# Two more batches of q transposed by DMA, in an attention and channel-mix kernel on one core

## The chip, the cores and the metric

The kernel runs on one core of one Trainium2 chip. The metric is the device time of one execution in microseconds. One execution was also taken by the hardware profiler, and all views of the trace are of that one.

## The reference

The program computes an attention over 32 memory slots and feeds its result to a channel mix. Sizes are batch B = 8, heads H = 8, sequence S = 576, head size D = 64, memory slots M = 32, model width 512, hidden width 1024. Cut to what matters:

```python
a = softmax(phi, axis=2)                       # (8, 8, 576, 32)
k_m = einsum('bhsm,bhsd->bhmd', a, k)
v_m = einsum('bhsm,bhsd->bhmd', a, v)
attn = softmax(scale * q @ k_m.T)              # q: (8, 8, 576, 64)
x = (attn @ v_m), heads side by side           # (8, 576, 512)
x_prev = x shifted by one token
xk = mu_k * x + (1 - mu_k) * x_prev
xr = mu_r * x + (1 - mu_r) * x_prev
out = sigmoid(xr @ w_r) * (relu(xk @ w_k)**2 @ w_v)
```

Inputs and output are float32; the kernel's matmuls are on bf16.

## The kernel before

The work is cut into named steps. A step is written `who:name`. For a batch b (0 to 7), `b:exp` takes exp of phi; `b:kv` (or `k` and `v` apart) forms k_m and v_m with TensorE (L237); `b:z` the sums; `b:nk`, `b:nv` the scaling on VectorE; `b:tk` the transposed keys; `b:q0` and `b:q1` transpose q with 18 TensorE matmuls each (L339) and copy the result to the tile qT (L343); `b:qx` does the same by two DMA transposes that SyncE issues (L315), one for each half of the partitions; `b:s0`, `b:s1` are the scores (L358); `b:l0` to `b:l3` the sums of the second softmax (L372); `b:w0`, `b:w1` the weights; `b:x0`, `b:x1` the values (L288); then the mixing steps. Batches 0 and 1 use variants with halves (`qh0`, `hn0`, `ht0`, `mr0`, `mk0`) to begin early. For the channel mix, `c<chunk>:<fi>` is one of eight hidden tiles of a chunk of 512 tokens (L520 to L528), `g:<t>` the gate of a tile of 128 tokens (L543), and `o:<t>` its output (L565 to L568), which ends in two stores that SyncE issues (L505).

Nothing is reordered by a scheduler: the list PLAN is one written-out order, and each step appends its instructions to the queues of the engines that it uses, each of which runs in its own order. A word `p:...` issues an early load, `b:load` (L291) issues the loads of batch b + 2, in the order that LOADS names. All loads of batches 1 to 7 are issued by GpSimd, cast float32 to bf16 on the way for q, k and v, and wait until their buffer is free: k, v, q and phi have two buffers each, for even and odd batches. The tile qT has three buffers, the output tile o four, and all PSUM tiles share eight banks. In before, `qx` is used for batches 6 and 7, and `q0`, `q1` for 1 to 5.

The DMAs of one kind share eight semaphores in turn, so that a DMA also waits for the landing of the DMA eight places ahead of it. `b:hold` (L263) is not used in before. The lines that a sentence can't say:

```python
def cross_q():
    for hg in range(2):
        nc.sync.dma_start_transpose(out=q_tile()[:, hg],
                                    in_=qs[b % 2][ROWS[hg]].rearrange("p n d -> p (n d)"))
def hold():
    spare = work.tile([1, 2], BF16, name="spare", tag="spare", bufs=1)
    nc.gpsimd.tensor_copy(spare, st["qT"][0:1, :, 0, 0])
```

`keep_busy` (L191, step `busy2`) issues two matmuls on zeros at the start; `mub` and `mu` (L198, L206) prepare the mixing vectors.

Of the kernel before, what the change touches and what calls it, by code (L numbers as in the profile page):

```python
# [15 lines left out]


PLAN = [
    "p:q:0a p:k:0b 0:exp1 0:exp0 0:k0c 0:z 0:qh0 0:k1c 0:hn0 0:ht0 0:s0 p:q:0b 0:hn1 p:v:0a 0:qh1 0:l0 0:ht1 0:l1",
    "0:s1 0:mub p:v:0b 0:l2 p:wr:0-4 p:wk:0-4 0:h1z 0:v0c 0:h0z 0:nr0 0:v1c p:phi:1 0:h2z 0:l3 0:y1 0:y0 p:wk:4-8",  # L20
    "0:h3z 0:nr1 0:busy2 0:y2 0:y3 0:nk0 0:nk1 0:mr0 0:mr1 0:mk0 0:mk1 c0:2a c0:0a g:2 1:exp c0:3a c0:2b c0:5b c0:4b",
    "g:3 1:z c0:6a g:0 p:k:1 1:k 1:nk c0:6b p:q:1 c0:7b c0:0b c0:3b 1:q0 1:q1 0:mu 1:tk c0:5a c0:1a c0:4a p:v:1 1:s1",
    "1:s0 c0:1b 1:v 1:l2 1:l0 c0:7a 1:nr0 p:wv:0-2 p:wv:2-4 1:nk0 1:h0z 1:l3 1:l1 1:h2z 1:nr1 1:h1z 1:h3z g:1 o:3a",
    "1:y2 1:y3 o:2a 1:nk1 1:y0 1:y1 o:2b o:3b 1:mk1 o:0a 1:mk0 1:mr0 c1:0 c1:2 c1:4 1:mr1 g:4 c1:6 c1:3 0:load 2:exp",
    "g:5 2:q0 2:q1 o:1a 7:load 2:z 2:kv 2:nk 2:nv o:0b 2:tk c1:1 2:s1 2:s0 c1:7 c1:5 2:l0 2:l2 2:l1 2:l3 2:r0z 2:r1z",
    "2:w0 2:w1 o:1b o:5 o:4 1:load 3:exp 2:x0 3:q0 g:6 3:z 3:q1 3:kv 2:x1 3:nk g:7 3:nv 3:tk 2:dd 2:k0d g:8 3:s0 3:s1",
    "2:load 2:k2d o:6 4:exp o:7 2:r0d 3:l0 c2:1 c2:5 3:l3 3:l2 4:z 3:l1 c2:0 3:r1z 3:w1 3:r0z 3:w0 c2:4 2:r2d c2:2",
    "c2:3 c2:7 3:x1 4:kv 3:load c2:6 3:x0 4:nk 4:nv g:10 3:dd 3:k0d g:11 3:k2d g:9 5:exp 4:tk 4:q1 4:q0 o:9 o:10 c3:7",
    "c3:0 o:8 5:z 4:s0 5:kv 4:load 3:r0d 4:s1 5:q1 6:exp 5:q0 6:qx 5:nk c3:5 c3:4 4:l1 3:r2d 4:l2 c3:3 5:nv 4:l3 4:l0",
    "5:tk 4:r1z c3:6 g:12 c3:2 6:z 6:kv 6:nv 5:s0 4:r0z 5:load 5:s1 4:w1 4:w0 c3:1 g:13 6:nk o:11 g:14 6:tk 4:x0 o:13",  # L30
    "4:x1 g:15 4:dd o:12 5:l3 4:k0d 5:l0 5:l1 5:r0z o:14 5:l2 4:k2d g:16 7:exp 4:r0d 5:r1z o:15 c4:1 c4:3 7:z 7:kv",
    "6:s1 5:w0 5:w1 6:s0 c4:5 c4:0 5:x0 7:nv 4:r2d 7:nk c4:2 6:l1 c4:4 c4:6 6:l2 c4:7 7:qx 6:l3 5:x1 5:dd g:18 5:k2d",
    "g:19 7:tk 6:l0 g:17 o:18 5:k0d 6:r1z o:16 o:19 7:s1 6:r0z 7:s0 c5:3 c5:1 c5:7 6:w0 g:20 7:l2 c5:2 6:w1 7:l0 7:l1",
    "c5:6 7:l3 5:r2d c5:0 c5:5 c5:4 7:r1z 5:r0d 6:x1 o:17 6:x0 g:21 7:r0z 6:dd 6:k2d o:20 o:21 7:w1 g:22 6:k0d g:23",
    "7:w0 o:23 o:22 6:r2d c6:2 7:x1 c6:5 c6:1 6:r0d 7:x0 c6:4 g:24 7:dd c6:0 6:load c6:7 c6:3 c6:6 g:25 g:26 7:k0d",
    "7:r0d 7:k2d g:27 o:25 o:24 o:26 c8:0 c7:5 c8:6 7:r2d g:28 o:27 g:29 c7:6 c7:0 c7:4 c8:2 g:30 c7:1 c7:2 c7:7 c7:3",
    "g:31 c8:7 c8:4 o:29 c8:3 o:28 o:31 g:32 c8:5 o:30 c8:1 g:33 g:34 o:33 g:35 o:32 o:34 o:35",
]

LOADS = {None: ("phi", "k", "v", "q"), 2: ("phi", "k", "q", "v"), 3: ("phi", "k", "q", "v"), 4: ("phi", "k", "q", "v")}  # L40
PRE = "k:0a id:"
SUMS = ()

# [6 lines left out]
def kernel(  # L50
# [64 lines left out]
    def load_batch(b):  # L115
        for what in LOADS.get(b, LOADS[None]):
            if what == "phi":
                load_phi(b, nc.gpsimd)
            elif what == "q":
                load_q(b)  # L120
            else:
                load_rows(kvs[b % 2][:, "kv".index(what)], (k, v)["kv".index(what)][b])
# [498 lines left out]
```

## Time and profile before

| what | value |
|---|---|
| median of three runs (lowest, highest) | 209.61 us (209.15, 209.96) |
| the profiled execution | 208.39 us, span 206.6 us, TensorE clock 0.999 |
| TensorE busy | 193.9 us, 94% of the span |
| ScalarE, VectorE, GpSimd busy | 159.5, 135.4, 29.4 us |
| bytes moved by DMA | 32.49 MB, of which 20.91 MB on the queue that GpSimd feeds |
| TensorE transposes of q, L339 | 180 matmuls, 190 ns each by the trace |
| VectorE copies of them, L343 | 18, 451 ns each |
| DMA transposes, L315 | 4 |

The span runs from the first to the last instruction; the execution's own time is 1.8 us longer. Matmuls are pipelined, so the sum of the means of single matmuls is more than the time that a group takes; the chain that ended last shows the latter. The trace gives the load of the DMA engines in slices and in windows, by queue: queue 0 is the one that GpSimd feeds, queue 1 the one that SyncE feeds. A DMA's time "to landing" runs from its issue.

### The profile page before, as it was taken

Reading aid. Unit: us, or ns where it says so; the run is one execution under the profiler, and the core shown is the slowest. Engines: PE = TensorE matmul, PEld = TensorE weight load, DVE = VectorE, ACT = ScalarE, POOL = GpSimd, SP = SyncE. Lnnn points to the kernel's source line nnn. Section 1 sums busy time; section 2 is a strip of 40 time slices with the busy share of each in tenths; the row PEclk is TensorE's granted clock in tenths of the full one; section 3 lists DMA queues with packets and bytes.
Section 4 is the critical chain, followed back from the end, with each engine's and each line's share of the span. In section 5 each row is a group of like instructions: output and inputs, shape, how many; then the busy total and the mean of one; then the engine's idle time right before and its main releaser. Section 6 shows DMA issues by size and latency. Waiting matters only on the chain.

```text
span 206.6 us, 5609 instructions
## 1 busy us (share of the span) xinstructions
PE 193.9 (94%) x2269; PEld 103.5 (50%) x2269; DVE 135.4 (66%) x364; ACT 159.5 (77%) x314; POOL 29.4 (14%) x45
## 2 busy tenths in 40 slices
PE   0499999999999999999999999999999999999992
PEld 0355676746555545466445764444434444444451
DVE  1129445866478989988749779487978944533232
ACT  3256899978778999978999799989878955882570
POOL 7652422201414102150000000000000000000000
PEclk9999999999999999999999999999999999999999
DMA  6999999999999999999999850502260062004335
GB/s 161 173 204 262 210 208 202 261 230 285 215 273 239 256 279 213 260 231 307 208 157 211 126 87 16 124 17 52 54 154 0 0 152 54 0 0 112 91 71 135
DMA packets 29274, 32.49 MB, mean 157 GB/s; under 512 B 6704, under 2 KB 24384, under 8 KB 29248
## 3 DMA queue, kind: packets, MB, share of 16 engines
q0 software_dynamic: 17392, 20.91, 53.8%
q1 hardware_dynamic: 11088, 10.37, 23.3%
q10 hardware_dynamic: 768, 0.85, 1.3%
q8 instruction: 18, 0.29, 0.6%
q14 instruction: 8, 0.07, 0.1%
HBM read 38.28 MB, written 9.44 MB: 231 GB/s over the span
## 4 chain that ended last, share of the span: by engine, by line
PE 92%; DMA 3%; POOL 1%; DVE 1%; issue 1%; POOLq 0%; DVEq 0%
PE pk L520 31%; PE pv L565 31%; PE pr L543 15%; PE kvps L237 4%; DMA kv<-in_k_dram 3%; PE mxps L288 2%; PE zps L372 2%; PE scps L358 2%; PE qtps L339 2%; PE nops L288 2%; PE zps L247 1%; PE ktps L301 1%; PE mub L200 1%; PE qtps L326 1%; DVE o L567 0%
## 5 line engine op out<-in xcount | busy, mean ns | idle before, releaser
L520 PE MATMUL pk<-xkT,wk 128*128 128x512 bf16 (+4 forms) x352 | 69.0, 341 | 0.0
L565 PE MATMUL pv<-wv,sq 128*128 128x512 bf16 (+1 forms) x328 | 66.2, 353 | 0.0
L528 DVE TENSOR_TENSOR sq<-rl 128x512 bf16<-128x512 bf16 (+5 forms) x104 | 32.7, 341 | 33.3 <-ACT rl L524 32.5
L524 ACT ACTIVATE rl<-pk 128x512 bf16<-128x512 f32 (+3 forms) x80 | 42.9, 560 | 13.4 <-PE pk L520 10.6
L520 PEld LDWEIGHTS <-wk 128*128 128x128 bf16 x352 | 32.7, 98 | 27.8 <-issue 1.6
L565 PEld LDWEIGHTS <-sq 128*128 128x128 bf16 x328 | 31.5, 98 | 29.9 <-issue 0.5
L543 PE MATMUL pr<-wr,xrT 128*128 128x512 bf16 x144 | 35.8, 380 | 0.0
L567 DVE TENSOR_TENSOR o<-sg,pv 128x512 f32<-128x512 f32 (+1 forms) x41 | 24.9, 620 | 15.0 <-PE pv L565 8.7
L548 ACT ACTIVATE sg<-pr 128x512 f32<-128x512 f32 x36 | 21.5, 610 | 8.8 <-PE pr L543 8.8
L543 PEld LDWEIGHTS <-xrT 128*128 128x128 bf16 x144 | 13.5, 98 | 14.8 <-issue 0.2
L550 ACT ACTIVATE sg<-sg 128x1024 f32<-128x1024 f32 x18 | 19.0, 1057 | 0.6
L551 ACT ACTIVATE sg<-sg 128x1024 f32<-128x1024 f32 x18 | 19.0, 1057 | 0.6
L401 ACT CAST x<-nops 128x320 bf16<-128x320 f32 (+1 forms) x48 | 15.7, 419 | 2.4 <-PE nops L288 2.3
L237 PE MATMUL kvps<-kv,em 64*32 64x128 bf16 (+1 forms) x720 | 8.7, 218 | 7.8 <-DMA kv<-in_k_dram 7.8
L423 DVE TENSOR_SCALAR mu_d<-diff,mu 128x576 bf16<-128x576 bf16 x48 | 15.5, 364 | 0.1
L362 ACT ACTIVATE e<-scps 128x320 bf16<-128x320 f32 (+1 forms) x32 | 11.0, 415 | 4.3 <-PE scps L358 4.2
L389 DVE TENSOR_TENSOR atn<-e,lz 128x576 bf16<-128x576 bf16 (+2 forms) x20 | 12.0, 631 | 1.4 <-ACT lz L382 1.3
L377 ACT ACTIVATE lz<-zps 128x320 f32<-128x320 f32 (+1 forms) x32 | 11.7, 413 | 0.8 <-PE zps L372 0.8
L237 PEld LDWEIGHTS <-em 64*32 64x32 bf16 x720 | 7.5, 95 | 8.9 <-ACT em L225 6.1
L225 ACT ACTIVATE em<-ph 128x1152 bf16<-128x1152 f32 (+1 forms) x9 | 9.4, 1056 | 2.3 <-DMA ph<-in_phi_dram 2.3
L382 ACT ACTIVATE lz<-lz 128x576 f32<-128x576 f32 (+2 forms) x20 | 11.1, 587 | 0.1
L413 DVE TENSOR_TENSOR diff<-x 128x1024 bf16<-128x1024 bf16 (+1 forms) x18 | 9.0, 552 | 2.4 <-ACT x L401 2.4
(65 smaller groups left out, 143.7 us busy)
## 6 DMA issues: line engine op xcount, KB each, us to landing
out_dram<-o SPq DMA_DIRECT2D x61, 128.0 KB, 2.4
ph<-in_phi_dram POOLq DMA_DIRECT2D x7, 576.0 KB, 15.7
kv<-in_k_dram POOLq DMA_DIRECT2D x7, 576.0 KB, 15.8
q<-in_q_dram POOLq DMA_DIRECT2D x7, 576.0 KB, 17.9
kv<-in_v_dram POOLq DMA_DIRECT2D x7, 576.0 KB, 19.3
out_dram<-o SPq DMA_DIRECT2D x18, 64.0 KB, 5.5
wk<-in_moe_w_k_dram POOLq DMA_DIRECT2D x2, 512.0 KB, 14.8
wv<-in_moe_w_v_dram POOLq DMA_DIRECT2D x2, 512.0 KB, 20.3
```

Of the source, the lines that this page charges most:

```text
L237: nc.tensor.matmul(kvps[c][g * M:(g + 1) * M], lhsT=em[ROWS[c], j, g, :], rhs=kv5[ROWS[c], parts, g, j, :], start=j == 0, stop=j == NJ - 1 ...
L401: nc.scalar.copy(st["x"][:, i, sl], pss[i])
L423: nc.vector.tensor_scalar_mul(t[:, i], st["d"][:, pr + i, :], mu1[:, o:o + 1])
L520: nc.tensor.matmul(pk[:, p0 - lo:p1 - lo], lhsT=wk_sb[:, di, fi * 128:(fi + 1) * 128], rhs=xk_T[:, di, p0 % RING:p0 % RING + p1 - p0], sta ...
L524: nc.scalar.activation(rl, pk, AF.Relu)
L528: nc.vector.tensor_mul(sq[:, fi, p:p + p1 - p0], rl[:, p0 - lo:p1 - lo], rl[:, p0 - lo:p1 - lo])
L543: nc.tensor.matmul(pr, lhsT=xr_T[:, di, c0:c0 + 128], rhs=wr_sb[:, di, :], start=(di == 0), stop=(di == ND - 1))
L548: nc.scalar.activation(sg[:, t % 2], pr, AF.Exp, scale=-1.0)
L550: nc.scalar.activation(sg, sg, AF.Ln, bias=1.0)
L551: nc.scalar.activation(sg, sg, AF.Exp, scale=-1.0)
L565: nc.tensor.matmul(pv[:, cols], lhsT=sq[:, fi, p:p + 128], rhs=wv_sb[:, fi, cols], start=(fi == 0), stop=(fi == NF - 1))
L567: nc.vector.tensor_mul(o[:, cols], gated[t // 2][:, t % 2, cols], pv[:, cols])
```

## The change

The steps `4:q0`, `4:q1`, `5:q0`, `5:q1` are replaced by `4:qx` and `5:qx`. LOADS no longer names batches 3 and 4, so that these load phi, k, v, q in this order, like the later ones. `4:hold` and `5:hold` are added: a copy of two elements on GpSimd that reads qT of that batch. The order of all steps in PLAN is new; at the start, `busy2` becomes `busy4`, phi of batch 1 is loaded before the weights, and `mu` moves forward. No function is changed.

```diff
 PLAN = [
-    "p:q:0a p:k:0b 0:exp1 0:exp0 0:k0c 0:z 0:qh0 0:k1c 0:hn0 0:ht0 0:s0 p:q:0b 0:hn1 p:v:0a 0:qh1 0:l0 0:ht1 0:l1",
-    "0:s1 0:mub p:v:0b 0:l2 p:wr:0-4 p:wk:0-4 0:h1z 0:v0c 0:h0z 0:nr0 0:v1c p:phi:1 0:h2z 0:l3 0:y1 0:y0 p:wk:4-8",
-    "0:h3z 0:nr1 0:busy2 0:y2 0:y3 0:nk0 0:nk1 0:mr0 0:mr1 0:mk0 0:mk1 c0:2a c0:0a g:2 1:exp c0:3a c0:2b c0:5b c0:4b",
...
-    "2:w0 2:w1 o:1b o:5 o:4 1:load 3:exp 2:x0 3:q0 g:6 3:z 3:q1 3:kv 2:x1 3:nk g:7 3:nv 3:tk 2:dd 2:k0d g:8 3:s0 3:s1",
-    "2:load 2:k2d o:6 4:exp o:7 2:r0d 3:l0 c2:1 c2:5 3:l3 3:l2 4:z 3:l1 c2:0 3:r1z 3:w1 3:r0z 3:w0 c2:4 2:r2d c2:2",
-    "c2:3 c2:7 3:x1 4:kv 3:load c2:6 3:x0 4:nk 4:nv g:10 3:dd 3:k0d g:11 3:k2d g:9 5:exp 4:tk 4:q1 4:q0 o:9 o:10 c3:7",
-    "c3:0 o:8 5:z 4:s0 5:kv 4:load 3:r0d 4:s1 5:q1 6:exp 5:q0 6:qx 5:nk c3:5 c3:4 4:l1 3:r2d 4:l2 c3:3 5:nv 4:l3 4:l0",
-    "5:tk 4:r1z c3:6 g:12 c3:2 6:z 6:kv 6:nv 5:s0 4:r0z 5:load 5:s1 4:w1 4:w0 c3:1 g:13 6:nk o:11 g:14 6:tk 4:x0 o:13",
-    "4:x1 g:15 4:dd o:12 5:l3 4:k0d 5:l0 5:l1 5:r0z o:14 5:l2 4:k2d g:16 7:exp 4:r0d 5:r1z o:15 c4:1 c4:3 7:z 7:kv",
-    "6:s1 5:w0 5:w1 6:s0 c4:5 c4:0 5:x0 7:nv 4:r2d 7:nk c4:2 6:l1 c4:4 c4:6 6:l2 c4:7 7:qx 6:l3 5:x1 5:dd g:18 5:k2d",
...
+    "p:q:0a 0:exp1 0:exp0 0:k0c 0:z 0:hn0 p:k:0b 0:qh0 0:ht0 0:k1c 0:s0 p:q:0b 0:mub 0:l0 p:v:0b 0:hn1 p:v:0a p:phi:1",
+    "0:qh1 0:ht1 0:l1 0:s1 p:wr:0-4 0:v0c 0:nk0 0:nr0 0:v1c 7:load 0:h0z p:wk:0-4 0:mu 0:h1z p:wk:4-8 0:l3 0:l2 0:y1",
+    "0:busy4 0:y0 0:h3z 0:nr1 0:h2z 0:nk1 0:y3 1:exp 0:y2 0:mr1 0:mr0 0:mk0 0:mk1 g:2 g:3 g:0 c0:3b c0:0a c0:1a c0:5b",
...
+    "c1:2 c1:3 c1:0 g:5 2:z 2:q1 2:q0 2:kv 2:nk o:0a 3:exp o:1a 2:tk o:1b 2:s1 2:s0 c1:6 2:load 2:l2 2:nv c1:7 2:l3",
+    "2:l1 2:l0 2:r1z 3:z 2:r0z 2:w1 2:w0 4:qx o:4 o:5 2:x0 3:kv 3:nk 3:nv g:6 3:tk 3:q1 3:q0 2:x1 g:7 2:dd g:8 2:k0d",
+    "o:7 2:k2d 2:r2d 3:s0 3:s1 3:load o:6 4:exp 3:l1 2:r0d 3:l2 3:l3 3:r1z 3:l0 c2:6 c2:3 3:w1 c2:5 c2:4 3:r0z 3:w0",
+    "c2:0 c2:2 g:10 4:z 4:kv 4:nk 5:qx 3:x0 4:nv c2:7 c2:1 3:x1 3:dd 4:tk 3:k0d g:9 3:k2d 3:r2d 5:exp g:11 o:11 o:8",
+    "4:load o:9 c3:0 6:exp c3:5 g:12 4:hold c3:7 5:kv 4:s0 4:s1 3:r0d c3:1 c3:2 c3:4 5:z 4:l3 4:l2 c3:6 4:r1z c3:3",
+    "4:l0 5:nk 5:nv 4:w1 g:13 4:l1 4:r0z o:10 5:tk o:13 6:z 4:w0 5:s0 6:kv 5:s1 6:nv 6:nk g:14 5:load 4:x0 5:l3 o:12",
+    "5:l1 4:x1 7:exp 6:qx g:16 g:15 4:dd 4:k0d 5:l2 4:k2d 5:r1z o:14 7:z 5:l0 6:tk o:15 c4:1 c4:0 5:r0z 5:w1 5:w0",
+    "6:load c4:4 c4:7 6:s1 6:s0 7:qx 4:r0d 7:kv 4:r2d c4:3 6:l2 7:nv c4:6 5:x1 c4:2 c4:5 g:18 5:x0 g:19 g:17 7:nk",
+    "7:tk 6:l0 6:l3 5:dd 5:k0d 6:r1z o:18 5:k2d o:17 6:l1 6:w1 o:19 c5:3 7:s1 7:s0 c5:0 o:16 6:r0z 7:l3 7:l2 6:w0",
...
+    "c6:5 c6:4 g:27 7:r0d g:25 c7:6 c7:2 o:27 o:25 o:26 g:30 c7:1 o:24 7:r2d c7:3 c7:7 c8:3 c7:4 c7:0 c8:1 5:hold",
...
 ]
 
-LOADS = {None: ("phi", "k", "v", "q"), 2: ("phi", "k", "q", "v"), 3: ("phi", "k", "q", "v"), 4: ("phi", "k", "q", "v")}
+LOADS = {None: ("phi", "k", "v", "q"), 2: ("phi", "k", "q", "v")}
```

## The prediction

> **What bounds the kernel now.** I read four views in this order: the page's busy shares and slices, the chain that ended last, the DMA view cut into short windows, and the queues of GpSimd (loads) and SyncE (stores, transposes).
>
> ```profile
> PE 193.9 (94%) x2269; PEld 103.5 (50%) x2269; DVE 135.4 (66%) x364; ACT 159.5 (77%) x314; POOL 29.4 (14%) x45
> DMA  6999999999999999999999850502260062004335
> PE 92%; DMA 3%; POOL 1%; DVE 1%; issue 1%; POOLq 0%; DVEq 0%
> PE kvps L237 <- DMA kv<-in_k_dram: 7.8, 2, 7.1
> 81.78 0.63 PE qtps L339 x36
> 90.69 0.65 PE qtps L339 x36
> L343 DVE COPY qT<-qtps 128x576 bf16<-128x576 bf16 x18 | 7.1, 451 | 0.4 <-PE qtps L339 0.4
> ```
>
> TensorE is the chain: 92% of it, and its only long wait is the first load. From about 15 us on it hardly pauses. But the DMA row is at 9 through slice 22, so until about 110 us the DMA engines are full too. The lines at 81.78 and 90.69 are the transposes of q4 and q5 on TensorE, which the change removes.
>
> What a DMA transpose does beside full loads is seen once before, for batch 6 (I call a batch's pair T4 to T7):
>
> ```profile
> 98.20 1.60 SPq L315 DMA_TRANSPOSE qT<-q  x1
> 99.90 4.71 SPq L315 DMA_TRANSPOSE qT<-q  x1
> 104.71 1.72 SPq L505 DMA_DIRECT2D out_dram<-o  x1
> out_dram<-o SPq DMA_DIRECT2D x1, 128.0 KB, 7.8
> ...
> DMA packets 321, 0.18 MB, mean 184 GB/s; under 512 B 207, under 2 KB 321, under 8 KB 321
> q0 software_dynamic: 117, 0.13, 75.7%
> q1 hardware_dynamic: 204, 0.05, 47.6%
> ...
> qT<-q SPq DMA_TRANSPOSE x2, 4.7
> ```
>
> The issue of T6 holds SyncE's queue 98.2 to 104.6. The packet lines are the window 105 to 106: queue 1, which SyncE feeds for transposes and stores, moves only small packets. Counts of small packets by windows of 1 us start at 102 (118, 144, 188, 204 a us) and stop at about 110.5: T6 takes 12.3 us, of which 3.8 pass before its first packet. The first store behind it lands at 104.7 + 7.8 = 112.5. T7, issued at 115.5 with no loads left, lands in 4.5 to 4.9 us from each issue, both by 121.5: 6 us.
>
> [...] from 102 to 109 both queues move, and the store waits behind T6. [...] The trace says 6 alone and 12.3 loaded, and I take the trace. [...]
>
> **The change part by part.**
>
> *Transposes of q4 and q5 on TensorE go:* 0.63 + 0.65 = 1.28 us, all on the chain. Their eight copies go from VectorE: 8 x 0.451 = 3.6 us, off the chain, worth 0.
>
> *Startup placed anew.* Two more idle matmuls: 2 x 0.43 = 0.85 us (before: 0.85 for two) if nothing covers them; `mu` moved here takes 0.15 out of the later run; first scores can come about 0.5 earlier because `ht0` precedes `k1c`, but the f32 `mub` (1.2 us) now precedes `qh1` and delays the second scores about as much. phi1 is loaded before the weights, which delays wr (landed 5.55 + 12.3 = 17.9) by some 1.5 us, while the first gate is due at about 21.5. Bounds -1 and +1; I take 0.
>
> *q last in batches 3 and 4:* v3 moves ahead of q3 (landed 61.3 and 58.3) and they swap; 3:q1 is due at 63. v4 and q4 swap too. Worth 0, covered by the loads that already stand in line.
>
> *The hold.* Its tiny copy (nearest row: GpSimd memsets, 0.10 to 0.23 us) waits for T4, and the loads of batch 7 stand behind it. But the load just ahead of it, q6 into q4's buffer, must itself wait for T4. So it adds 0 to 0.2 us to a queue, nothing to the chain. `5:hold` comes after all loads: 0. That the hold holds anything is thus the part of the change that I expect not to happen.
>
> *T4 and T5 on SyncE's queue* is the costly part. Adding the chain's piece durations in the new PLAN order, from the first gate at 21.5, and 1.4 for the small gaps (the same addition puts before's 5:kv at 88.4, and the chain shows it at 89.86), TensorE is due at 5:kv 90.4, 4:s0 91.1, 5:s0 101.2, 6:s1 115.1.
>
> T4 stands in SyncE's queue ahead of the stores of o:4, o:5, o:7, o:6. It waits for q4. In before the last load of batch 4 landed at 53.7 + 19.4 = 73.1; four tiles of stores (1.05 MB) now come later instead, and stores slow the loads by about 0.19 MB per 0.58 (windows 92 to 96), so 1.7 us less: 71.5. Loads of batch 5 are queued all the while, unlike T6, whose last part ran as the loads dried up. The bounds of T4's duration are 12.3 (as T6) and 3.8 + 2048 packets / 150 per us = 17.5. I take 15: T4 lands at 86.5 and the store of o:4 at 88.3. VectorE meets o:11, which needs the buffer of o:4 (four buffers), at about 83.5: it stands 4.8 us, with everything behind it. A PSUM bank of 5:kv waits for o:11 (done 89.0), those of 4:s0 and 4:s1 for o:8 and o:9 (89.7, 90.3): just in time. TensorE loses 0 to 0.5; at 17.5 it would lose 3.
>
> T5 waits for q5 (batch 5's last load landed 85.9 before; about 86 now) and, since eight semaphores rotate, for o:4's store: issue 88.3, landing 103.3. 5:s0 is due 101.2: 2.1 us lost. The stores of o:11 and so on stand behind T5, so o:13 waits for o:11's buffer until about 105, and the bank of g:14 waits for o:13: another 1.2. Together 3.3.
>
> T6 now stands behind the store of o:12: due 107, with the delay 111. The loads, which ended at 109.5, are pushed back by T4 and T5. T6 cost the loads 0.76 MB over 102 to 109.5, that is 3.8 us; with loads plentiful I take 3 each, so they end at 115.5. T6 then needs some 9 us, between 6 and 12.3, and lands at 120; 6:s1 is due 115.1 + 3.3 = 118.4: 1.6 lost. T7 comes after the loads; 7:s1 is at 128 or later, so 0.
>
> The sum: -1.3 + 0 + 0.2 + 3.3 + 1.6 = +3.8. The profiled execution is 208.39 (span 206.6 and 1.8 around it), which gives 212.2; the three runs' median of 209.61 gives 213.4. I say 212.9.
>
> **The rivals.**
>
> *The transposes hide (faster).* All four pairs land before their scores, and only the 1.28 is left, with a little from the startup: about 208.3. For it: 15 to 17 us lie between q4's landing and 4:s0 or between q5's and 5:s0, more than T6's 12.3, and VectorE is relieved by 3.6. Against it: T6 has only 8 us between its place in the queue and 6:s1. It decides where a loaded pair takes under 8 us there and under 13 before.
>
> *Each pair takes 17.5 (much slower).* T4 lands at 89, VectorE stands until 91.7 (3 lost), T5 lands at 108.8 (4.6 and 1.2 lost), T6 runs after the loads: -1.3 + 0.2 + 8.8 = +7.7, 217.3. For it: loads never run dry under T4 and T5. Against it: the rate of small packets rose while T6 ran.
>
> *Gain and loss cancel:* T5 lands in time, T6 costs 1 to 2: about 209.8.
>
> **How the numbers follow.** A measurement of this kernel can tell some 0.5% (1 us) from no change. Chances: loss as forecast, +1.1 to +7: 0.53; over that: 0.12; cancelled within 0.5%: 0.09; hidden, faster: 0.26. So slower 0.65. The forecast alone spans 210.7 to 216.5. The range reaches down into the hidden case to 207.9, and up to 216.8, which leaves most of the 17.5 case out.
>
> **What the profile after would show.** Right: two fewer L339 runs of 36 on TensorE and DMA_TRANSPOSE x8; SyncE waiting at L315 for q from about 61 to 71; VectorE's L567 waiting for a DMA near 84 to 89; TensorE's L358 waiting on DMA qT near 101 and 115; the loads' end past 113. Wrong: no L358 wait on qT, or transposes that land within 8 us beside loads. If a startup line grows by over 1 us, my 0 there failed.

## The result and the profile after

The changed kernel takes 224.47 us (median of 4 executions, 222.77 to 225.6) against 209.38 (208.32 to 209.96): ratio 1.072, interval 1.064 to 1.080. The forecast was 212.9 in a range of 207.9 to 216.8: the direction was right, the loss of 15 us is some four times the one forecast. The profiled execution took 225.6 us, with a span of 223.8. The ratios below leave out executions that lie more than 1.5% above the fastest of their kernel: two of four in the first run with idle matmuls in the pauses, its profiled one among them, and one of four in the second.

The page first: busy shares, the slices of TensorE, its granted clock and the DMA engines, and the shares of the chain that ended last.

```profile
PE 199.5 (89%) x2199; PEld 104.6 (47%) x2199; DVE 131.8 (59%) x356; ACT 160.0 (71%) x314; POOL 29.6 (13%) x47
PE   0599979999999999329958999999999999999993
PEclk9999999999999999965995999999999999999998
DMA  6999999999999999999999569044025004302625
PE 67%; DMA 22%; ACT 6%; issue 2%; SPq 1%; POOL 1%; DVE 1%; POOLq 0%; DVEq 0%
```

The rows of TensorE and its clock before:

```profile
PE   0499999999999999999999999999999999999992
PEclk9999999999999999999999999999999999999999
```

TensorE's row was full from slice 2 on (slices are counted from 0, each 5.6 us); now it has two deep dents, in slices 16 to 17 (90 to 101 us) and 20 (112 to 117), and at or just after each of them the granted clock falls, to 0.6 and 0.5 in slices 17 and 18 and to 0.5 in slice 21. The small one in slice 5 comes up with the first experiment. TensorE has fewer matmuls and yet is busy 5.6 us longer, because some of them run at a lower clock: 0.50 was granted from 100 to 104 us. In the chain DMA went from 3% to 22%.

The queue of SyncE (start, duration, engine and line) and what the chain holds of DMA show the two pairs:

```profile
72.12 11.49 SPq L315 DMA_TRANSPOSE qT<-q  x2
83.70 12.44 SPq L505 DMA_DIRECT2D out_dram<-o  x8
96.24 8.76 SPq L315 DMA_TRANSPOSE qT<-q  x2
105.09 20.84 SPq L505 DMA_DIRECT2D out_dram<-o  x12
126.10 3.40 SPq L315 DMA_TRANSPOSE qT<-q  x2
```

```profile
73.58 22.07 DMA qT<-q
...
97.62 19.31 DMA qT<-q
116.94 0.04 issue
116.98 0.55 PE scps L358 x4
```

T4 is issued at 72.1 and lands at 95.6, 23.5 us later. T5 is issued at 96.24 and lands at 116.94, 20.7 us. T6, issued at 126.1 when the loads are over, has landed by 132.3, 6.2 us later. Issuing alone holds SyncE's queue for 11.5 and 8.8 us. The wait tables name who paid (us in total, times, longest):

```profile
PE kvps L237 <- DVE o L567: 6.0, 1, 6.0
PE scps L358 <- DMA qT<-q: 2.2, 1, 2.2
PE scps L358 <- DVE o L567: 1.5, 2, 1.1
PE pk L520 <- issue: 1.2, 1, 1.2
PE pr L543 <- DVE o L567: 0.9, 1, 0.9
PE pk L520 <- ACT sg L548: 0.2, 1, 0.2
```

```profile
DVE o L567 <- DMA out_dram<-o: 10.3, 3, 8.6
```

None of these rows stood in before. The path is the one that the prediction drew: T4 holds SyncE's queue, the store of o:4 stands behind it (its halves are issued from 83.7 and land 12.3 and 12.6 us later, right after T4, so they wait behind T4's packets too), VectorE stands in o:11 for the buffer that this store reads and starts nothing else for 8.65 us, to 97.04, and TensorE stands in 5:kv for the PSUM bank that o:11 reads. TensorE's waits for T4 and what stood behind it sum to 6.0 + 1.5 + 0.2 = 7.7 us, those for T5 to 2.2 + 0.9 = 3.1: 10.8 us. The wait for the DMA eight places ahead shows as well: the last of the eight stores behind T4 was issued at 95.67, just as T4 landed, after SyncE had stood 6.4 us for it.

### The profile page after: what moved, and what is told of

Read it like the earlier page. It is cut to its first block, busy times and chain, and to the rows that moved or that the text cites. A ratio compares the mean times of both kernels' runs of the same rounds, so it can differ in the third digit from the quotient of the medians.

```text
span 223.8 us, 5467 instructions
## 1 busy us (share of the span) xinstructions
PE 199.5 (89%) x2199; PEld 104.6 (47%) x2199; DVE 131.8 (59%) x356; ACT 160.0 (71%) x314; POOL 29.6 (13%) x47
## 4 chain that ended last, share of the span: by engine, by line
PE 67%; DMA 22%; ACT 6%; issue 2%; SPq 1%; POOL 1%; DVE 1%; POOLq 0%; DVEq 0%
PE pk L520 22%; PE pv L565 22%; DMA qT<-q 18%; PE pr L543 12%; DMA kv<-in_k_dram 3%; PE kvps L237 2%; PE mxps L288 2%; PE zps L372 2%; PE scps L358 1%; PE nops L288 1%; ACT sg L550 1%; SPq L315 1%; ACT lz L377 1%; PE qtps L339 1%; PE idle L195 1%
## 5 line engine op out<-in xcount | busy, mean ns | idle before, releaser
L520 PE MATMUL pk<-xkT,wk 128*128 128x512 bf16 (+4 forms) x352 | 70.7, 349 | 1.4 <-issue 1.2
L565 PE MATMUL pv<-wv,sq 128*128 128x512 bf16 (+1 forms) x328 | 68.1, 358 | 0.1
L524 ACT ACTIVATE rl<-pk 128x512 bf16<-128x512 f32 (+3 forms) x80 | 42.2, 561 | 18.4 <-PE pk L520 16.9
L520 PEld LDWEIGHTS <-wk 128*128 128x128 bf16 x352 | 33.5, 99 | 31.5 <-issue 5.5
L567 DVE TENSOR_TENSOR o<-sg,pv 128x512 f32<-128x512 f32 (+1 forms) x41 | 24.9, 618 | 29.5 <-PE pv L565 10.5
L548 ACT ACTIVATE sg<-pr 128x512 f32<-128x512 f32 x36 | 21.4, 604 | 17.9 <-DVE o L567 12.3
L237 PE MATMUL kvps<-kv,em 64*32 64x128 bf16 (+1 forms) x720 | 9.5, 227 | 13.8 <-DMA kv<-in_k_dram 7.7
L237 PEld LDWEIGHTS <-em 64*32 64x32 bf16 x720 | 8.1, 98 | 15.4 <-issue 8.2
L377 ACT ACTIVATE lz<-zps 128x320 f32<-128x320 f32 (+1 forms) x32 | 12.2, 414 | 3.0 <-PE zps L372 3.0
L382 ACT ACTIVATE lz<-lz 128x576 f32<-128x576 f32 (+2 forms) x20 | 11.3, 598 | 0.2
## 6 DMA issues: line engine op xcount, KB each, us to landing
ph<-in_phi_dram POOLq DMA_DIRECT2D x7, 576.0 KB, 15.1
wv<-in_moe_w_v_dram POOLq DMA_DIRECT2D x2, 512.0 KB, 20.7
```

The source lines that it names most:

```text
L237: nc.tensor.matmul(kvps[c][g * M:(g + 1) * M], lhsT=em[ROWS[c], j, g, :], rhs=kv5[ROWS[c], parts, g, j, :], start=j == 0, stop=j == NJ - 1 ...
L520: nc.tensor.matmul(pk[:, p0 - lo:p1 - lo], lhsT=wk_sb[:, di, fi * 128:(fi + 1) * 128], rhs=xk_T[:, di, p0 % RING:p0 % RING + p1 - p0], sta ...
L524: nc.scalar.activation(rl, pk, AF.Relu)
L548: nc.scalar.activation(sg[:, t % 2], pr, AF.Exp, scale=-1.0)
L565: nc.tensor.matmul(pv[:, cols], lhsT=sq[:, fi, p:p + 128], rhs=wv_sb[:, fi, cols], start=(fi == 0), stop=(fi == NF - 1))
L567: nc.vector.tensor_mul(o[:, cols], gated[t // 2][:, t % 2, cols], pv[:, cols])
```

## The experiments

Twelve kernels ran. Ratios are to the kernel before, run on the same chip in the same set. The diffs show the words of PLAN around an edit, from the changed kernel unless said otherwise.

### The new order with q4 and q5 left on TensorE

```diff
-2:w0 4:qx o:4 ... 4:nk 5:qx 3:x0 ... 4:tk 3:k0d ... 4:hold c3:7 ... 5:tk o:13 ... 5:hold
+2:w0 o:4 ... 4:nk 3:x0 ... 4:tk 4:q0 4:q1 3:k0d ... c3:7 ... 5:tk 5:q0 5:q1 o:13
```

> The new order and load order of after, but q4 and q5 transposed by TensorE (18 + 18 matmuls a batch, right after the transposed keys), no holds. Theory (transposes that land 21 to 23 us after issue hold the scores, hold the stores behind them, and the pause lowers the TensorE clock): no pause above 2 us, clock 0.99 or more, 210 to 212 us; the 1.5 us that after had lost by 45 us of the trace stays. Rival (the new order is slow in itself, whoever transposes): 217 us or more.

210.27 us, ratio 1.0061 (1.0038 to 1.0084, 20 executions). So the order and the start cost 1.3 us by this ratio, and the transposes with their holds the other 14, near enough. Where the order loses is visible by stretches of 15 us (TensorE's busy time is the second number of a row, after the stretch's length); the first row is of before, the second of the changed kernel:

```profile
30.00:45.00 15.00, 14.95 (x276) 10.12 (x275) 11.23 (x35) 13.53 (x35) 2.98 (x4) 1.00 1.28 229
```

```profile
30.00:45.00 15.00, 13.60 (x283) 9.26 (x281) 10.43 (x32) 12.51 (x33) 2.98 (x4) 1.00 1.28 225
```

TensorE loses 1.35 us there in the changed kernel, of which 1.2 is one pause in the middle of an L520 group that waited for nothing the profile shows ("issue"; 1.8 in this run). It stands in the wait table of every kernel with the new order, between 0.7 and 1.9 us long, and not in before. Its cause is open.

### Only T5, and only T4

```diff
-2:w0 4:qx o:4 ... 4:tk 3:k0d ... 4:hold c3:7
+2:w0 o:4 ... 4:tk 4:q0 4:q1 3:k0d ... c3:7
```

> After, but q4 by TensorE; q5 stays with DMA. Theory: the pair of batch 5 is issued near 86 and lands about 108, 5:s0 is due near 103, so about 5 us of wait, 1 more behind a store and 3 at the lower clock: 217 to 220 us. Rival (the pair of batch 4 alone is the cause, and the second only suffers from its delay): 212 us or less.

220.8 us, ratio 1.0552 (1.0494 to 1.0611): a little more than expected. One pair at its second place costs nearly as much as both: T5 is issued at 85.7 instead of 96.2, and lands at 110.3, 24.6 us later, so 5:s0 waits 5.6 us and a gate 2.0 for a bank that VectorE holds in L567.

```diff
-4:nk 5:qx 3:x0 ... 5:tk o:13 ... 5:hold
+4:nk 3:x0 ... 5:tk 5:q0 5:q1 o:13
```

> After, but q5 by TensorE; q4 stays with DMA. Theory: VectorE and TensorE stand near 91 to 98 as in after (6 us at 5:kv, 1.5 at the scores), then 3 us at the lower clock, then nothing: 218 to 221 us. Rival (the pair of batch 5 is the cause): 212 us or less.

217.34 us, ratio 1.0402 (1.0342 to 1.0463), slightly under the expectation. The wait table repeats the two lines of the changed kernel for T4, 6.0 us at 5:kv and 8.6 us of VectorE at L567. So the two costs do not add: 7.1 for T4 alone and 10.5 for T5 alone, over the 210.27 of the first run, against 14.2 for both. With both, T5 took 20.7 us instead of 24.6, and T4's pause delays TensorE, which gives T5 more time until its scores are due.

### The stores first, the transposes behind them

```diff
-2:w0 4:qx o:4 ... 3:load o:6 4:exp ... 4:nk 5:qx 3:x0 ... 4:load o:9 c3:0
+2:w0 o:4 ... 3:load o:6 4:qx 4:exp ... 4:nk 3:x0 ... 4:load o:9 5:qx c3:0
```

> After, but the pair of batch 4 stands in SyncE's queue behind the stores of o:4, o:5, o:7, o:6 instead of ahead of them, and that of batch 5 behind those of o:11, o:8, o:9. Its issue stays near 72, when q4 lands. Theory (two holds: late qT, and blocked stores): the wait of VectorE for a store and of 5:kv for VectorE is gone, but 4:s0, due near 92, waits for qT until about 96, and 5:s1 until about 117: 220 to 224 us. Rival (the blocked stores are the whole loss): 213 us or less.

216.32 us, ratio 1.0332 (1.0285 to 1.0378). Less than the theory said and more than the rival. VectorE's wait for a store is gone, and of TensorE's new waits one is left:

```profile
PE scps L358 <- DMA qT<-q: 4.2, 1, 4.2
```

This order is 8 us faster (224.47 - 216.32), and the waits behind stores, 6.0 + 1.5 + 0.9 us in the changed kernel, are gone. Not all of the 8 is theirs, since T5 changed too. T4 itself is no faster: issued at 76.6, it lands at 98.3, 21.7 us later, and 4:s0 waits for it. T5, issued at 95.2, lands 11.5 us later: the load of q6, which needs the buffer that T4 reads, had held GpSimd's queue, so few loads ran beside T5 (none of their packets from 98 to 102 us). It cost no wait.

### The loads held while the pairs run

```diff
-3:load o:6 ... 4:load o:9 ... 4:hold c3:7 ... c8:1 5:hold
+4:hold 3:load o:6 ... 5:hold 4:load o:9 ... c3:7 ... c8:1
```

> After, but each hold stands ahead of the next batch's loads: 4:hold before the loads of batch 5, 5:hold before those of batch 6, so that the loads stop until the pair has landed. Theory (loads in flight make a pair slow): the pair of batch 4 lands within 6 to 9 us of its issue near 72, 5:kv waits no more for VectorE; the pair of batch 5 is as fast; but the loads of batch 6 then come late, 6:kv waits 4 to 7 us for them, and the clock falls: 214 to 219 us. Rival (a pair takes some 20 us by itself, loads or not): its landing stays 19 us or more after issue, and the time is 224 us or more.

226.83 us, ratio 1.088 (1.084 to 1.092). The landing is as the theory said, the total is not. T4 now takes 6.3 us from its issue at 72.2, T5 6.0. One wait has taken the place of all the others:

```profile
PE scps L358 <- ACT rl L524: 16.5, 1, 16.5
```

ScalarE, which must free the bank, stood in 6:exp for phi of batch 6, and GpSimd issued that load at 102.1, behind the hold for T5 and so behind a q5 that was itself late (issued at 81.4 behind the first hold, landed at 94.7). This shows the two halves of the matter. What makes a pair slow is the loads beside it: the same pair takes 6.3 us without and 23.5 with them. And the time of which the loads are deprived comes back.

The packets of single microseconds show it. Four windows of 1 us: first the changed kernel at 77 and 85, then this run at 74, then the run with the stores first at 87. A row is queue, packets, MB, share of the DMA engines:

```profile
q0 software_dynamic: 139, 0.16, 91.5%
q1 hardware_dynamic: 141, 0.04, 27.2%
...
q0 software_dynamic: 24, 0.03, 96.2%
q1 hardware_dynamic: 19, 0.00, 38.3%
```

```profile
q1 hardware_dynamic: 580, 0.15, 99.3%
```

```profile
q0 software_dynamic: 26, 0.04, 40.8%
q1 hardware_dynamic: 30, 0.01, 32.8%
```

With both queues at work they move packet for packet at 77 us, one small transpose packet (some 260 bytes by this run's 0.15 MB / 580) against one of a load (some 1,150 bytes). Without loads the transposes go four times as fast. The second pair of rows is something else: from 83 to 88 us the two queues together moved 178, 161, 43, 148 and 132 packets a us instead of 280, although the engines were counted busy.

The run with the stores first has the same stretch, at its lowest from 87 to 88 (the last two rows), and no store was under way there: the earlier ones were issued by 75.8 and moved their last packets in the us from 81, and the next was issued at 91.4. So stores are not needed for it. In both runs it sets in while the loads' queue moves packets of over 2 KB: 29, 34 and 37 of them in the three us from 81 in the changed kernel, as this row of the us from 82 shows (329 - 295), and 27, 29, 34 and 24 in the four from 83 with the stores first.

```profile
DMA packets 329, 0.25 MB, mean 248 GB/s; under 512 B 272, under 2 KB 295, under 8 KB 329
```

From 80 to 88 us the changed kernel moved 128 of them (1496 - 1368 in that window), and a load of 576 KB in 128 packets has 4.5 KB in each, a row of the phi tile (1152 float32): I take them for phi of batch 6, the one load of a batch that is not cast (issued at 72.9). No run takes phi out of the stretch, so this is a candidate and not a shown cause; the pair T6 of before has a slow us as well (217 packets of both queues from 108 to 109), with none over 2 KB in it.

### Idle matmuls in the pauses, to price the clock

```diff
-c3:7 5:kv ... 6:kv 5:s1
+c3:7 4:busy24 5:kv ... 6:kv 4:busy14 5:s1
```

> After, with 24 idle matmuls on zeros put ahead of 5:kv and 14 ahead of 5:s1, where TensorE stands. Theory (the pause lowers the clock, and that costs some 6 us of after's 15): the waits remain, with landings as in after, the clock between 90 and 125 us of the trace stays at 0.9 or more, and the time falls to 217 to 221 us. Rival (the clock is a by-product, the waits are all): 223 to 227 us.

225.99 us median; the two executions that count took 222.21 and 223.14, ratio 1.0663 (1.0609 to 1.0718). That is some 1 us under the changed kernel, with intervals that overlap, and not the 217 to 221 expected. Waits of 1 to 2.4 us were left behind the fills in the trace, but it is of one of the other executions (228.85), so this run settles nothing. A longer fill tells more:

```diff
-c3:7 5:kv ... 6:kv 5:s1
+c3:7 4:busy36 5:kv ... 6:kv 4:busy26 5:s1
```

> The changed kernel with 36 idle matmuls (8 us at full clock) ahead of 5:kv and 26 (5.7 us) ahead of 5:s1, in place of the 24 and 14 of the run before, after which waits of 1 to 2.5 us had stayed and the clock had fallen. The fill takes a PSUM bank of its own, so 5:kv and the scores behind it get the next bank and wait for the next output tile; the fill is long enough to cover that. Theory (the low clock after a pause of TensorE cost about 6 us of the 15): no wait over 1 us behind the fills, the granted clock stays above 0.95 from 90 to 130 us, 218 to 221. Rival (the clock costs under 2 us): 223 or more with the clock held.

226.17 us median, ratio 1.0782 (1.0682 to 1.0882), and the clock stood at 1.00 throughout the profiled execution. By the total the rival is right. But the fills were longer than the pauses: 5:kv starts 1.8 us later than in the changed kernel, and the gate behind 5:s1 2.5 later. Equal work in between tells the clock's price. TensorE's timeline (start, duration) of the changed kernel, and then of this one, at the first and last group of two stretches that hold the same matmuls:

```profile
101.55 5.20 PE L520 MATMUL pk<-xkT,wk 128*128 128x512 bf16 x12 [0.23 <-ACT sg L548]
...
111.62 0.28 PE L301 MATMUL ktps<-identity,kbd 128*128 128x128 bf16 x2
...
118.38 1.86 PE L543 MATMUL pr<-wr,xrT 128*128 128x512 bf16 x4 [0.94 <-DVE o L567]
...
128.32 0.27 PE L301 MATMUL ktps<-identity,kbd 128*128 128x128 bf16 x2
```

```profile
102.14 2.75 PE L520 MATMUL pk<-xkT,wk 128*128 128x512 bf16 x12 [0.16 <-ACT rl L524]
...
109.77 0.27 PE L301 MATMUL ktps<-identity,kbd 128*128 128x128 bf16 x2
...
120.86 1.04 PE L543 MATMUL pr<-wr,xrT 128*128 128x512 bf16 x4
...
128.77 0.27 PE L301 MATMUL ktps<-identity,kbd 128*128 128x128 bf16 x2
```

From the first to the second: 10.07 against 7.63 us. From the third to the fourth: 9.94 against 7.91. The low clock cost 2.4 + 2.0 = 4.5 us in these two stretches, less than the 6 expected. These rows show when the clock fell and came back; the granted clock of the changed kernel is the number before the last two:

```profile
96.00:100.00 4.00, 1.62 (x79) 1.01 (x79) 1.37 (x2) 0.00 (x0) 2.35 (x5) 0.54 1.27 180
100.00:104.00 4.00, 2.92 (x14) 1.06 (x14) 3.10 (x7) 2.85 (x7) 0.74 (x2) 0.50 1.15 171
104.00:108.00 4.00, 4.00 (x23) 1.77 (x22) 1.36 (x4) 1.84 (x5) 0.00 (x0) 0.68 1.16 200
```

By 0.54 the clock went to half at about 96.3, some 4.5 us into the pause of 6.0 us that ended at 97.78. By 0.68 the full clock was back at about 106.6: 8.8 us after TensorE's return at 97.78 and 5 after 101.55, from where it worked without a pause. The second fall came at about 116.8 (0.69 over the 2 us from 116), when TensorE had been idle for 2 us, since 114.76. What length of pause brings a fall these two do not settle.

### T4 behind the stores, with the loads held for it

```diff
-2:w0 4:qx o:4 ... 3:s1 3:load o:6 4:exp ... 4:nk 5:qx 3:x0 ... 4:hold c3:7 ... 5:tk o:13 ... 5:hold
+2:w0 o:4 ... 3:s1 p:phi:5 o:6 4:qx 4:hold 3:load 4:exp ... 4:nk 3:x0 ... c3:7 ... 5:tk 5:q0 5:q1 o:13
-LOADS = {None: ("phi", "k", "v", "q"), 2: ("phi", "k", "q", "v")}
+LOADS = {5: ("k", "v", "q"), None: ("phi", "k", "v", "q"), 2: ("phi", "k", "q", "v")}
```

> The kernel of e1_q45_on_pe (new order, q5 by TensorE), but q4 by DMA, its pair behind the stores of o:4 to o:7 in SyncE's queue, and the loads of k, v, q of batch 5 held until it has landed; phi of batch 5 is loaded before that. Theory: the pair lands 6 to 9 us after issue, hides, and saves the 0.65 us of q4 on TensorE: 209 to 210.5 us. Rival (the pause in the loads comes back at 5:kv or 6:kv): over 211.5 us.

216.5 us, ratio 1.0362 (1.0321 to 1.0403); the rival was right. T4 takes 6.3 us, nobody waits for it or for a store, but 4:s1 waits 5.3 us for ScalarE, which stands in 6:exp for phi of batch 6. The same in the order of before, with only q4 by DMA:

```diff
-o:6 4:exp o:7 2:r0d ... 4:kv 3:load c2:6 ... 4:tk 4:q1 4:q0 o:9
+o:6 4:exp o:7 4:qx 2:r0d ... 4:kv p:phi:5 4:hold 3:load c2:6 ... 4:tk o:9
```

(LOADS gets the same row for batch 5.)

> The kernel before, with its own order, but q4 by DMA, the pair behind the store of o:7 in SyncE's queue, and the loads of k, v, q of batch 5 held until it has landed. Theory: 0.65 us less of TensorE, of which a part is lost where 6:kv waits for loads that come 4 to 6 us later (it had 3.5 us to spare): 208.7 to 210 us. Rival (loads that come late cost more than is saved): over 211 us.

214.43 us, ratio 1.0274 (1.0235 to 1.0312); again the rival. Small waits for phi (4.7 us of ScalarE), for a q and a v (2.1 and 1.4 us of TensorE) come back. Then phi of batch 6 was moved ahead of the hold:

```diff
-3:s1 p:phi:5 o:6 4:qx 4:hold 3:load 4:exp
+3:s1 p:phi:5 o:6 4:exp p:phi:6 4:qx 4:hold 3:load
-LOADS = {5: ("k", "v", "q"), None: ("phi", "k", "v", "q"), 2: ("phi", "k", "q", "v")}
+LOADS = {5: ("k", "v", "q"), 6: ("k", "v", "q"), None: ("phi", "k", "v", "q"), 2: ("phi", "k", "q", "v")}
```

> As the run with T4 behind the stores and the loads held for it (q5 on TensorE, 216.5), but phi of batch 6 is loaded ahead of the hold, as soon as 4:exp has freed its buffer. Theory (that run's loss was ScalarE waiting for phi of batch 6 behind the held loads, 5.3 us, with the clock's fall after it): no wait of ScalarE for phi over 1 us, 210 to 212.5. Rival (the pause of the loads comes back as another late tensor, k, v or q of batch 6 or 7, whatever its order): 214 to 217 with that wait in the table.

216.1 us, ratio 1.0347 (1.0273 to 1.0420): no gain. The wait for phi is gone, and 6:s1 waits instead:

```profile
PE scps L358 <- DMA qT<-q: 4.0, 1, 4.0
```

T6 was issued at 111.1, while the late loads still ran, and landed 11.8 us later. In the run with phi unmoved it was issued at 117.1, with 19 load packets left in that us and none after, and nothing waited for it. Three orders of one held pair thus give 214 to 217, each with another late tensor.

### Without the holds

```diff
-4:hold c3:7 ... c8:1 5:hold
+c3:7 ... c8:1
```

> The changed kernel without 4:hold and 5:hold. Theory (the load of q6, ahead of the hold, must itself wait for T4, and 5:hold stands after all loads, so they hold nothing): 223.5 to 225.5, with GpSimd still waiting for T4 and T5 at L107. Rival (the holds stop other loads, and those are what costs): 220 or less.

226.32 us, ratio 1.0819 (1.0743 to 1.0895), which overlaps that of the changed kernel; the median is 0.8 above the theory's figure. The load of q6 waits for T4 until 96.74, with the hold until 96.21. Taking the holds away gains nothing, and the load ahead of the first one waits for T4 either way, as the theory says.

### Two idle matmuls at the start instead of four

```diff
-0:busy4 0:y0
+0:busy2 0:y0
```

(on top of the first run of this section)

> The changed kernel's order with q4 and q5 on TensorE (210.27 before) and two idle matmuls at the start where it has four. Theory (the start costs 0.85 us for two idle matmuls that nothing covers): 209.4. Rival (they lie in a gap in which TensorE waits anyway): 210.3, and the pause of TensorE in an L520 group near 32 us stays in both.

210.96 us, ratio 1.0081 (1.0041 to 1.0122), not below the 1.0061 with four. The theory is refuted. TensorE's timeline at the first gates, here and then in the changed kernel:

```profile
21.35 4.46 PE L543 MATMUL pr<-wr,xrT 128*128 128x512 bf16 x12
```

```profile
21.51 2.75 PE L543 MATMUL pr<-wr,xrT 128*128 128x512 bf16 x12
```

Two idle matmuls fewer take 0.85 us less (1.06 against 1.91), but the values after them (L288) take 3.64 us against 2.83, and then the gates 1.7 longer, near the pace at the low clock (12 matmuls of the same shape took 5.20 us at a granted 0.50, above). This is one profiled execution of each.

No version beat the kernel before.

## Why the prediction was right or wrong, point by point

**The forecast's direction and its path were right.** T4 was issued at 72.1 (said: 71.5), TensorE came to 5:kv at 91.5 (90.4), o:11 was where VectorE stood, a bank of 5:kv where TensorE stood, and g:14 lost 0.9 (1.2). The run without T4 and T5 puts 14 of the 15 us on them.

**The term that failed is the duration of a pair: 15 us, with an upper bound of 17.5.** It was 23.5 for T4 and 20.7 for T5. Put T4's 23.5 into the prediction's own chain: landing at 95.6, the store and o:11 by 97.7, TensorE due at 91.5, so 6.2 lost; measured 6.0. Three things in the step were wrong. The first is the number of packets. Queue 1 in the pages before and after:

```profile
q1 hardware_dynamic: 11088, 10.37, 23.3%
q1 hardware_dynamic: 15824, 11.55, 26.4%
```

Two pairs more are 4736 packets more, 2368 a pair, where the bound counted 2048, a number that no view of before shows. Its 150 packets a us beside full loads were nearly right (about 140, from 77 to 80 us). With both corrected, 3.8 + 2368 / 140 makes 20.7 and not 17.5. The second is that I took 15, below the bound, because T6 had gone faster; T6 had run into the end of the loads, which I knew and let pull the number down. (T7, read as 6 us alone, took 6.3.) The third is what no bound contained: the stretch from 83 to 88 us, in which queue 1 moved 382 packets where 140 a us would have been 700. By my estimate from these that is 2.3 us, most of the 2.8 that T4 is past 20.7. Its cause is open. That T5 took just 20.7 proves nothing: its packets set in sooner after its issue, and it had a slow us of its own (35 and 32 packets from 105 to 106).

**T5:** predicted to be issued at 88.3 and to cost 3.3 us in waits; issued at 96.24, costing 3.1. The agreement is luck: T5 ended 13.6 us late, and T4 had delayed the scores about as much.

**A term was missing: the clock.** A TensorE that stood 6 us was slow afterwards (0.50 granted from 100 to 104 us). At 4.5 us, by equal work and not by a total, it is larger than the whole forecast loss, and the pause that it follows was forecast as 0 to 0.5, so that the question did not come up. The row PEclk of before, all nines, came with no such pause and could not price one.

**The startup, taken as 0 with bounds of 1, was 1.3** by the ratio of the run with q4 and q5 on TensorE (0.8 to 1.8 by its interval), at the bound or past it. What can be seen of it is none of the things priced: taking two idle matmuls away gained nothing, and TensorE loses 1.35 us in 30 to 45 us, for which there was no term. That pause is open.

**T6, 1.6 us, was 0.** TensorE had been delayed so long that T6 ran after the loads.

**Not contradicted:** the hold (0.18 us on GpSimd, and taking it away gains nothing), and the order of q and v, for which no wait shows. The 1.28 us for the transposes on TensorE was not measured apart.

The sum with what was measured: -1.3 for TensorE's transposes, +10.8 of waits, +4.5 of clock, +1.3 of order make 15.3; the medians differ by 15.1, the spans of the two profiled executions by 17.2, of which the order's own profiled execution, 2.3 above that of before, accounts for 1 more; 0.9 of that execution stays unexplained.

**The rivals.** "The transposes hide" said that it decides where a loaded pair takes under 8 us at 6:s1 and under 13 before; it took over 20. "Each pair takes 17.5", with 217.3, was nearest and still 7 us short, for the same two terms. The runs with held loads show that a pair can land in 6 to 6.5 us, but only by stopping loads that are themselves on a deadline.

## What to carry to other kernels

A transfer that moves many small packets should be costed by counting them, at the rate at which the queues alternate (here about 140 a us for each), and with the queue beside it full: here a pair took 23.5 us beside loads and 6.3 without, and the 1.28 us of TensorE that it saved had been the cheaper way. Before a transfer is put into a queue ahead of stores, follow what those stores free: here a buffer, then VectorE, which started nothing else for 8.65 us, then a PSUM bank. And where a forecast includes a pause of TensorE of several us, add the slow matmuls after it, here 4.5 us after waits of 10.8 in all.

## What the runs showed of the hardware that was not expected

- A transpose queue and a casting load queue shared the DMA engines packet for packet: 141 to 139 in 1 us, though the bytes were 0.04 to 0.16 MB; alone the transposes moved 580 (the changed kernel at 77 us, the run with the loads held at 74).
- About 5 us of a pair beside loads in which the two queues moved 43 to 178 packets a us instead of 280, while the engines were counted busy (96% and 38% at the lowest). It came without a store near it too. Not explained.
- Issuing the second transpose of a pair kept SyncE from its stores for 10.0 us beside loads in the changed kernel and 11.3 in the run with the stores first; the issue of a whole pair took 3.6 us without loads.
- The granted clock fell to half in two pauses of TensorE in the changed kernel: some 4.5 us into one, at 96.3, and 2 us into the other, at 116.8. About 10 us later it was full again the first time, at 106.6.
- With two idle matmuls in place of four the first gates took 4.46 us instead of 2.75, while the windows gave a granted clock of 1.00 there. In the changed kernel the trace's first record of the clock is at 21.2 us, and the windows from 15 us on give 1.00 ahead of it all the same: for the start that row says nothing.
